# A product of weights whose second operand is loaded twice, once turned, and elementwise work moved up in the planner's order

## Chip, cores, metric

One core of a Trainium2 chip. The metric is the device time of one execution in microseconds, the median of three runs. Engines are named TensorE (PE; its weight loads are PEld), VectorE (DVE), ScalarE (ACT), GpSimd (POOL) and SyncE (SP, which issues most DMAs).

## What is computed

Three blocks in a row, on 2304 tokens of 512 features. First an attention with random features (4 batches, 8 heads, 576 positions, 64 per head, 128 features). Then a normalized, gated feed-forward layer. Then a mixture of eight experts, where every token goes to the expert that a global sort of all token and expert scores assigns to it, at most 288 tokens an expert.

```python
q_p, k_p = phi(q_s), phi(k_s)                  # exp of a projection by omega
kv = einsum('bhsm,bhsd->bhmd', k_p, v);  z = sum(k_p, axis=2)
x = (q_p @ kv) / (q_p @ z + 1e-6)              # then heads side by side: (2304, 512)

xn = x / rms(x) * rms_g
g = xn @ w_gate                                # (512, 1536)
h = g * sigmoid(g) * (xn @ w_val)
x = h @ w_out                                  # (1536, 512)

logits = x @ moe2_w_gate                       # (512, 8)
order = argsort(-logits.flatten())             # greedy: token to expert, 288 each
out[mask_e] = relu(x[mask_e] @ w1[e]) @ w2[e]
```

The weights of the feed-forward layer arrive as 64-bit floats, as pairs of 32-bit words.

## The kernel before

The program is written in a framework that places instructions by a planner. TensorE's order is the program's own during the first part; ScalarE, VectorE, GpSimd and SyncE get theirs from the planner, which simulates the run and gives each engine, among the instructions that it holds ready, the one with the highest priority. Priority is the place in the program; `tc.high_priority(offset=n)` moves a block n instructions ahead. On the chip each engine then works through its list in order. Buffers of a pool are taken and given back as their last reader ends.

Precision: an operand of a big matmul is split into a high part (float32r) and the rest, and three matmuls make one product.

The first part is a loop over 81 ticks, `run_tick`. Each tick works on 76 items of attention (40 for keys, 36 for queries), each item passing through up to six lags, one a tick. In a tick stand, in TensorE's order: the units of weight conversion (`conv_pe`), attention (`it.pe`), and a step of the feed-forward layer's first product (`ffn_step_pe`). From tick 23 on (`FFN_AT`) three ticks of ten have a second step, so there are 1.3 steps a tick. Attention's elementwise work has `AHEAD_A = 200`; that of a step (`ffn_el`) and that of the units (`conv_el`) have no offset.

A unit loads 512 KB of 64-bit weights into one of three "ws" buffers (`load`, always three units ahead). At lag 0 ScalarE takes the magnitude of the upper word (L570), at lag 1 VectorE builds a 32-bit float from the two words with three instructions (L574 to L576, held behind attention's last maximum by `issue_after`). The first 24 units are the gate and value weights: at lag 2 ScalarE and GpSimd split them (L599, L600) into a slab that the steps read. The 12 `WoUnit`s are w_out: at lag 1 the 32-bit float goes to a scratch tensor in HBM (`wo_dr`); at lag 2 TensorE transposes four blocks of 128 by 128 (L614) into a PSUM buffer "gv" and ScalarE copies them back (L629); at lag 3 TensorE multiplies them by the router's weights (L618) into the same buffer, and VectorE copies the 128 by 8 product out in two instructions (L631, L632) as `wog`. So w_out times the router's weights exists, and the router's scores come from h with eight columns (`ffn_lg`). Units start at 0.5 a tick up to tick 23, then 0.9 until all 24 first ones have started, then 0.7.

A step is twelve matmuls (L644, L645, L647) for one slab of 128 of the 1536 features and gate or value, on a block of 512 tokens (four and a half blocks), into a "gv" buffer; the pool has two of them, shared with the units:

```python
psG = ctx.enter_context(tc.tile_pool(name="psG", bufs=2, space=PSUM))
```

After a gate step ScalarE takes tanh (L656) and VectorE multiplies (L657, which gives "gv" back). After a value step VectorE multiplies (L665 in the first block, which then stores h by SyncE at L667; L669 in the others, followed by ScalarE L671, GpSimd L672 and the store L673). A block's first step needs its slab converted (`gvs`), and, one slab later, its `wog` (`wogs`). Steps that are left when attention is done follow in a loop of their own, with `wo_split`, which loads the scratch back and splits it for the second product. After that come the routing, filled with the second product's matmuls, and the experts; the change does not touch them.

Of the kernel before, what the change touches and what calls it, by code (L numbers as in the profile page):

```python
# [9 lines left out]
F32 = mybir.dt.float32  # L10
# [10 lines left out]
NT, DM, FF, E, FE = B * S, 512, 1536, 8, 1024  # L21
# [12 lines left out]
KD = DM // 128  # L34
KF = FF // 128
# [9 lines left out]
DW = 3  # L45
# [5 lines left out]
PACE = (0.5, 0.9, 0.7)  # L51
FFN_AT = 23
AHEAD_A = 200
HB = 6
LATE = 2

# [231 lines left out]


@with_exitstack  # L290
def kernel(ctx, tc, qT, kT, kC, v1, vC, om, wgv, rms, wo, wg2, w1, w2, cfd, trd, cid, out, dbg=None):
    nc = tc.nc
    dbg = dbg or {}
    keep = ctx.enter_context(tc.tile_pool(name="keep", bufs=1))
# [9 lines left out]
    ident = cf[:, C_ID:C_SL]  # L304
# [11 lines left out]
    wg2s = keep.tile([128, KD, E], F32, name="wg2s")  # L316

    xp = ctx.enter_context(tc.tile_pool(name="xp", bufs=2))
    psG = ctx.enter_context(tc.tile_pool(name="psG", bufs=2, space=PSUM))
    mid = ExitStack()  # L320
    fp = mid.enter_context(tc.tile_pool(name="fp", bufs=2))
# [6 lines left out]
    st = {}  # L328
# [73 lines left out]
    class KItem:  # L402
# [42 lines left out]
        def el(self, lag):  # L445
            b, p, g = self.b, self.p, self.g
            if lag == 0:
                self.ft = feat(self.pp, 128, 2 * len(self.ts))
            elif lag == 1 and g == 2:
                r, w = p // 2, b // 2  # L450
                if w not in kvs:
                    kvs[w] = at.tile([128, H, 2, D + 1], F32, name="kvs", bufs=1)
                nc.scalar.copy(kvs[w][:, 4 * r:4 * r + 4, b % 2, :].rearrange("p (o h) d -> p h o d", o=2),
                               st.pop(("pk", b, r))[:, :4 * (D + 1)].rearrange("p (h o d) -> p h o d", h=2, o=2))
# [148 lines left out]
    class WoUnit(Unit):  # L603
# [4 lines left out]
            return wo[self.f]  # L608

        def pe(self, lag):  # L610
            if lag == 2:
                self.pt = psG.tile([128, KD, 128], F32, name="gv")
                for k in range(KD):
                    nc.tensor.transpose(self.pt[:, k, :], self.t[:, k * 128:(k + 1) * 128], ident)  # L614
            elif lag == 3:
                self.pw = self.pt[:, 0, :E]
                for k in range(KD):
                    nc.tensor.matmul(self.pw, self.t[:, k * 128:(k + 1) * 128], wg2s[:, k, :], start=(k == 0), stop=(k == KD - 1))  # L618

        def el(self, lag):  # L620
            f = self.f
            if lag == 0:
                self.magnitude(fp.tile([128, DM], F32, name="dw", bufs=DW))
            elif lag == 1:
                with tc.issue_after(st["mx"].ins):
                    self.word()
                nc.sync.dma_start(wo_dr[f], self.t)
            elif lag == 2:
                nc.scalar.copy(self.t, self.pt.rearrange("p k m -> p (k m)"))  # L629
            elif lag == 3:  # L630
                nc.vector.tensor_copy(wog[:, f, 0, :], self.pw)  # L631
                nc.vector.tensor_sub(wog[:, f, 1, :], self.pw, wog[:, f, 0, :])  # L632
                wogs.add(f)
# [16 lines left out]
    def ffn_el(j, f, v, pg):  # L650
        n = WIDTH[j]
        nh = n // HB2
        if v == 0:
            fst["th"] = fp.tile([128, BLK], F32, name="th")
            th = fst["th"][:, :n]
            nc.scalar.activation(th, pg, AF.Tanh, scale=0.5)  # L656
            nc.vector.scalar_tensor_tensor(th, th, 1.0, pg, op0=OP.add, op1=OP.mult)  # L657
            return
        th = fst["th"][:, :n]
        hp = fp.tile([128, BLK // HB2, 2, HB2], F32R, name="hp")  # L660
        hf = hp.bitcast(F32)
        dst = h_dr[nh * j:nh * j + nh] if nh > 1 else h_dr[NT // HB2 - 1:]
        dst = dst[:, :, f].rearrange("b p x -> p b x")
        if j == 0:
            nc.vector.scalar_tensor_tensor(hf[:, :, 0], pg.rearrange("p (b t) -> p b t", b=nh), 0.5,  # L665
                                           th.rearrange("p (b t) -> p b t", b=nh), op0=OP.mult, op1=OP.mult)
            nc.sync.dma_start(dst[:, :, :HB2], hf[:, :, 0])  # L667
            return
        nc.vector.scalar_tensor_tensor(th, pg, 0.5, th, op0=OP.mult, op1=OP.mult)  # L669
        h = th.rearrange("p (b t) -> p b t", b=nh)  # L670
        nc.scalar.copy(hp[:, :nh, 0], h)  # L671
        nc.gpsimd.tensor_sub(hp[:, :nh, 1], h, hp[:, :nh, 0])  # L672
        nc.sync.dma_start(dst, hf[:, :nh].rearrange("p b l t -> p b (l t)"))  # L673
        fq.append((j, f, hp))
# [30 lines left out]
    def ffn_rank_el():  # L705
        for c0 in rks:
            ranks(nc, st["eng"], fp, cf[:, C_T:C_N].rearrange("p (a b) -> p a b", b=E), L, R, c0, 2)
        rks.clear()
# [14 lines left out]
    def ffn_step_el():  # L723
        if "el" in fst:
            j, f, v, pg = fst.pop("el")
            ffn_el(j, f, v, pg)
            ffn_rank_el()
            return j, f, v
        return None
# [3 lines left out]
    for b in range(B):  # L733
# [1 line left out]
        w, o = divmod(b, 2)  # L735
        items += [QItem(w * PAIR + c, hf) for c in range(o * (PAIR // 2), PAIR // 2 + o * (PAIR // 2 + 1))
                  for hf in range(2)]
    useq = [WgvUnit(f, g) for f in range(KF) for g in range(2)] + [WoUnit(f) for f in range(KF)]
    AHEAD = 3


# [36 lines left out]
    def conv_pe(pace):  # L778
        conv["due"] += pace
        conv["live"] = [(lag + 1, u) for lag, u in conv["live"] if lag < 3]  # L780
        while conv["due"] >= 1 and conv["next"] < len(useq):
            conv["due"] -= 1
            conv["live"].append((0, useq[conv["next"]]))
            conv["next"] += 1
        for lag, u in conv["live"]:
            u.pe(lag)
# [8 lines left out]
    def run_tick(tick):  # L795
        live = [(lag, items[tick - lag]) for lag in range(NLAG) if 0 <= tick - lag < len(items)]
        conv_pe(PACE[0] if tick < FFN_AT else PACE[1] if conv["next"] < 2 * KF else PACE[2])
        with tc.high_priority(offset=AHEAD_A):
            for lag, it in live:
                it.pe(lag)  # L800
        ffn_step_pe()
        for lag, it in live:
            if lag == 5 and isinstance(it, QItem) and it.hf and it.c * 128 // BLK not in xblk:
                while len(xblk) > 1:
                    ffn_step_el()
                    if not ffn_step_pe():
                        conv_el()
                        conv_pe(1)
        with tc.high_priority(offset=AHEAD_A):
            for lag, it in live:  # L810
# [52 lines left out]
    def ffn2_load(c, g):  # L863
        ht = f2.tile([128, 4, 2, 128], F32R, name="ht", bufs=HB)
        j, o = divmod(c * 128, HB2)
# [8 lines left out]
    def late_load(f):  # L874
        hs = f2.tile([128, 4, 2, 128], F32R, name="ht", bufs=HB)
        hs = hs.rearrange("p a l t -> p (a l t)").rearrange("p (b l t) -> p b l t", b=BLK // HB2, l=2)
# [11 lines left out]
    while True:  # L888
# [5 lines left out]
        j, f, v = ffn_step_el()  # L894
# [45 lines left out]
    def ffn2():  # L940
        for i, (c, g) in enumerate(seq2):
            if i + HB - 1 < len(seq2):
                ffn2_load(*seq2[i + HB - 1])
            if i % 6 == 2 and wcur[0] < LOADS:
# [207 lines left out]
def layouts(q, k, v, omega, moe_w_gate, moe_w_val, moe_w_out, moe_rms_g, moe2_w_gate, moe2_w1, moe2_w2):  # L1152
    a = np.asarray
    hp = H // 2

    def bits(x):
        return np.ascontiguousarray(x).view(np.int64)

    qT = a(q).reshape(B, hp, 2, S, D).transpose(2, 4, 1, 0, 3).reshape(128, hp, NC, 128).transpose(2, 0, 1, 3)
    kf = a(k).reshape(B, hp, 2, S, D).transpose(0, 1, 2, 4, 3).reshape(B, hp, 128, S)  # L1160
    kT = kf[..., :512]
    kC = kf[..., 512:].reshape(B, hp // 2, 2, 128, 64).transpose(0, 1, 3, 2, 4).reshape(B, hp // 2, 128, 128)
    vf = np.ones((B, hp, 2, S, D + 1), np.float32)
    vf[..., :D] = a(v).reshape(B, hp, 2, S, D)
    v1 = vf[:, :, :, :512].reshape(B, hp, 2, 4, 128, D + 1).transpose(0, 1, 4, 3, 2, 5)
    vC = np.zeros((B, hp // 2, 2, 64, 2, 2, D + 1), np.float32)
    for o in range(2):
        vC[:, :, o, :, :, o] = vf[:, o::2, :, 512:].transpose(0, 1, 3, 2, 4)
    vC = vC.reshape(B, hp // 2, 128, 2, 2 * (D + 1))
    om = np.zeros((128, 2 * M), np.float32)  # L1170
    om[:D, :M] = a(omega).T
    om[D:, M:] = a(omega).T
    wgv = np.stack([bits(moe_w_gate), bits(moe_w_val)], 0).reshape(2, KD, 128, KF, 128).transpose(3, 2, 0, 1, 4)
    wgv = wgv.reshape(KF, 128, 1024)
    rms = np.tile(a(moe_rms_g)[None], (128, 1))
    wo = bits(moe_w_out).reshape(KF, 128, DM)
    wg2 = a(moe2_w_gate).reshape(KD, 128, E).transpose(1, 0, 2)
    w1 = a(moe2_w1).reshape(E, KD, 128, 4, 256).transpose(0, 3, 2, 1, 4).reshape(E, 4, 128, 1024)
    w2 = a(moe2_w2).reshape(E, KE, 128, KD, 128).transpose(0, 3, 2, 1, 4).reshape(E, 4, 128, 1024)
    d = dict(qT=qT, kT=kT, kC=kC, v1=v1, vC=vC, om=om, wgv=wgv, rms=rms, wo=wo, wg2=wg2, w1=w1, w2=w2,  # L1180
             cf=const_f32(), tri=triangles(), ci=const_i32())
    return {n: np.ascontiguousarray(x) for n, x in d.items()}

# [16 lines left out]
```

## Time and profile before

| what | us |
| --- | --- |
| median of 3 runs | 931.28 |
| lowest, highest | 929.66, 931.54 |
| the profiled execution | 928.5 |
| its span, first to last instruction | 926.7 |

The span is what the profile shows; the rest of an execution lies around it. Busy time of TensorE is the union of its instructions' durations. Matmuls are pipelined, and the end of each is modelled, so one's duration reaches into the next; distances between starts tell what one takes of the engine's order. "Idle before" and the releaser in square brackets, or behind "<-", name what the engine had waited for.

### The profile page before, as it was taken

How to read it: one execution, taken by the hardware profiler on the slowest of the kernel's cores; microseconds unless marked ns; L12 is line 12 of the kernel's file. 1: busy time of each engine (PE TensorE's matmuls, PEld its weight loads, DVE VectorE, ACT ScalarE, POOL GpSimd, SP SyncE). 2: the span in 40 equal slices, each digit the busy share in tenths (PEclk: the TensorE clock that was granted, in tenths of full speed). 3: DMA queues.
4: the chain of work that ended last, by engine and by line, in shares of the span. 5: the costliest groups of instructions: out<-in, count | busy, mean ns of one | idle time of the engine just before them, and what ended most of it. 6: DMA issues, size and time to landing. Idle time of an engine off the chain costs nothing.

```text
span 926.7 us, 16209 instructions
## 1 busy us (share of the span) xinstructions
PE 905.5 (98%) x6219; PEld 786.7 (85%) x6219; DVE 526.7 (57%) x1226; ACT 373.4 (40%) x843; POOL 226.1 (24%) x298
## 2 busy tenths in 40 slices
PE   8998999999999999999999999999999999999996
PEld 7887888888888888877789777777779999999996
DVE  4799895555643354431263666666664665566661
ACT  5985575445544345333242100100013544444441
POOL 1355342122222323255333000000012222122111
PEclk9999999999999999999999999999999999999998
DMA  8556554454322121177674677676623666666650
GB/s 293 180 169 203 147 153 147 143 185 166 127 104 75 61 88 69 46 272 274 194 223 159 193 205 206 190 211 203 182 83 106 181 197 194 187 210 190 185 162 26
DMA packets 111486, 152.61 MB, mean 165 GB/s; under 512 B 6448, under 2 KB 70576, under 8 KB 111408
## 3 DMA queue, kind: packets, MB, share of 16 engines
q1 hardware_dynamic: 105600, 137.28, 47.3%
q0 software_dynamic: 3072, 9.44, 3.3%
q10 hardware_dynamic: 2736, 4.85, 1.4%
q8 instruction: 49, 0.80, 0.4%
q14 instruction: 29, 0.24, 0.1%
HBM read 107.50 MB, written 44.04 MB: 164 GB/s over the span
## 4 chain that ended last, share of the span: by engine, by line
PE 71%; issue 6%; DVE 2%; POOL 2%; DMA 1%; ACT 0%; POOLq 0%; DVEq 0%; ACTq 0%
PE py L955 16%; PE gv L644 8%; PE gv L645 8%; PE gv L647 8%; PE ph L1069 3%; PE ph L1066 3%; PE ph L1067 3%; PE py L1077 3%; PE py L1078 3%; PE py L1079 3%; PE cnt L180 2%; PE pm L496 1%; PE pm L439 1%; PE lg L684 1%; PE gv L618 1%
## 5 line engine op out<-in xcount | busy, mean ns | idle before, releaser
L644 PE MATMUL gv<-xh,wc 128*128 128x512 f32 (+1 forms) x480 | 180.3, 382 | 5.3 <-DVE th L657 4.7
L645 PE MATMUL gv<-xh,wc 128*128 128x512 f32 (+1 forms) x480 | 174.4, 370 | 0.0
L955 PE MATMUL py<-wc,ht 128*128 128x512 f32 x648 | 167.3, 404 | 0.0
L955 PEld LDWEIGHTS py<-wc,ht 128*128 128x128 f32 x648 | 114.9, 189 | 19.0
L647 PE MATMUL gv<-xl,wc 128*128 128x512 f32 (+1 forms) x480 | 118.4, 368 | 0.0
L644 PEld LDWEIGHTS gv<-xh,wc 128*128 128x128 f32 x480 | 90.6, 189 | 23.2 <-DVE th L657 6.3
L645 PEld LDWEIGHTS gv<-xh,wc 128*128 128x128 f32 x480 | 90.6, 189 | 13.7
L647 PEld LDWEIGHTS gv<-xl,wc 128*128 128x128 f32 x480 | 85.3, 189 | 15.7
L657 DVE SCALAR_TENSOR_TENSOR th<-th,gv 128x512 f32<-128x512 f32 (+1 forms) x60 | 37.9, 631 | 104.4 <-ACT th L656 104.1
L399 ACT ACTIVATE ft<-pp,mx 128x128 f32<-128x128 f32 x288 | 82.5, 374 | 18.1 <-DVE mx L396 17.4
L672 POOL TENSOR_TENSOR hp<-th,hp 128x512 fp32r<-128x512 f32 (+1 forms) x48 | 59.8, 1247 | 122.5 <-ACT hp L671 108.6
L926 DVE TENSOR_TENSOR wc<-ws,wc 128x512 fp32r<-128x512 f32 x128 | 84.8, 682 | 0.0
L1077 PE MATMUL py<-ehh,wc 128*128 128x288 f32 x256 | 77.7, 304 | 0.0
L1078 PE MATMUL py<-ehl,wc 128*128 128x288 f32 x256 | 75.9, 297 | 0.0
L1079 PE MATMUL py<-ehh,wc 128*128 128x288 f32 x256 | 75.8, 296 | 0.0
L1066 PE MATMUL ph<-exh,wc 128*128 128x288 f32 x256 | 71.7, 302 | 0.0
L1067 PE MATMUL ph<-exh,wc 128*128 128x288 f32 x256 | 69.8, 295 | 0.0
L966 ACT COPY ys<-py 128x512 f32<-128x512 f32 x18 | 10.6, 588 | 144.3 <-PE py L955 103.5
L936 ACT CAST wc<-ws 128x1024 fp32r<-128x1024 f32 x64 | 66.9, 1046 | 2.4 <-ACT ys L966 2.4
L656 ACT ACTIVATE th<-gv 128x512 f32<-128x512 f32 (+1 forms) x60 | 33.3, 555 | 73.2 <-PE gv L647 64.1
L396 DVE TENSOR_REDUCE mx<-pp 128x4 f32<-128x512 f32 (+1 forms) x76 | 50.0, 657 | 19.0 <-PE pp L392 9.8
L1071 DVE SCALAR_TENSOR_TENSOR ehl<-ph,ehh 128x288 fp32r<-128x288 f32 x64 | 29.3, 458 | 46.8 <-ACT ehh L1070 46.8
(217 smaller groups left out, 1696.4 us busy)
## 6 DMA issues: line engine op xcount, KB each, us to landing
ws<-in_w_dram SPq DMA_DIRECT2D x64, 512.0 KB, 4.0
ht<-h_dr SPq DMA_DIRECT2D x54, 512.0 KB, 4.1
h_dr<-hp SPq DMA_DIRECT2D x36, 512.0 KB, 2.8
ws<-in_wgv_dram SPq DMA_DIRECT2D x24, 512.0 KB, 4.2
h_dr<-hp SPq DMA_DIRECT2D x24, 256.0 KB, 2.5
ws<-in_wo_dram SPq DMA_DIRECT2D x12, 512.0 KB, 3.7
h_dr<-ht SPq DMA_DIRECT2D x12, 512.0 KB, 3.1
y_dr<-ys ACTq DMA_DIRECT2D x18, 256.0 KB, 4.3
```

What stands on the lines that cost most here:

```text
L399: nc.scalar.activation(ft[:n, g], pp[:n, g], AF.Exp, bias=mx[:n, g:g + 1])
L644: nc.tensor.matmul(pg[:, :n], w[:, 0, v, k], xh[:, k, :n], start=(k == 0), stop=False)
L645: nc.tensor.matmul(pg[:, :n], w[:, 1, v, k], xh[:, k, :n], start=False, stop=False)
L647: nc.tensor.matmul(pg[:, :n], w[:, 0, v, k], xl[:, k, :n], start=False, stop=(k == KD - 1))
L926: nc.vector.tensor_sub(w[:, 1, h], sv[:, h], w[:, 0, h])
L936: nc.scalar.copy(w[:, 0], sv)
L955: nc.tensor.matmul(py, ht[:, i4, a], w[:, l, f % 2], start=(f == 0 and n == 0), stop=(f == KF - 1 and n == 2))
L1066: nc.tensor.matmul(ph, w[:, 0, k, m], xh[:, k], start=(k == 0), stop=False)
L1067: nc.tensor.matmul(ph, w[:, 1, k, m], xh[:, k], start=False, stop=False)
L1077: nc.tensor.matmul(py, w[:, 0, k], hh[:, k], start=(k == 0), stop=False)
L1078: nc.tensor.matmul(py, w[:, 0, k], hl[:, k], start=False, stop=False)
L1079: nc.tensor.matmul(py, w[:, 1, k], hh[:, k], start=False, stop=(k == KE - 1))
```

## The change

A second copy of w_out, `woT`, is an input: each of its 12 pieces has the four blocks of 128 by 128 turned. A new `WoTUnit` loads it, makes magnitude and words as before, and at lag 2 multiplies it by the router's weights, with VectorE's two copies in the same lag. The `WoUnit` keeps load, magnitude, words and the store to the scratch tensor, and has no TensorE work any more. The list of units is 24, then 12 `WoTUnit`, then 12 `WoUnit`: 48 for 36. `ffn_el` gets an offset of 150.

```diff
+AHEAD_F = 150
@@ class WoUnit
         def pe(self, lag):
-            if lag == 2:
-                self.pt = psG.tile([128, KD, 128], F32, name="gv")
-                for k in range(KD):
-                    nc.tensor.transpose(self.pt[:, k, :], self.t[:, k * 128:(k + 1) * 128], ident)
-            elif lag == 3:
-                self.pw = self.pt[:, 0, :E]
-                for k in range(KD):
-                    nc.tensor.matmul(self.pw, self.t[:, k * 128:(k + 1) * 128], wg2s[:, k, :], start=(k == 0), stop=(k == KD - 1))
+            pass
 
         def el(self, lag):
             f = self.f
@@
+    class WoTUnit(Unit):
+
+        def __init__(self, f):
+            self.f = f
+
+        def src(self):
+            return woT[self.f]
+
+        def pe(self, lag):
+            if lag == 2:
+                self.pw = psG.tile([128, E], F32, name="gv")
+                for k in range(KD):
+                    nc.tensor.matmul(self.pw, self.t[:, k * 128:(k + 1) * 128], wg2s[:, k, :], start=(k == 0),
+                                     stop=(k == KD - 1))
+
+        def el(self, lag):
+            f = self.f
+            if lag == 0:
+                self.magnitude(fp.tile([128, DM], F32, name="dw", bufs=DW))
+            elif lag == 1:
+                with tc.issue_after(st["mx"].ins):
+                    self.word()
             elif lag == 2:
-                nc.scalar.copy(self.t, self.pt.rearrange("p k m -> p (k m)"))
-            elif lag == 3:
                 nc.vector.tensor_copy(wog[:, f, 0, :], self.pw)
                 nc.vector.tensor_sub(wog[:, f, 1, :], self.pw, wog[:, f, 0, :])
                 wogs.add(f)
@@ def ffn_step_el
-            ffn_el(j, f, v, pg)
+            with tc.high_priority(offset=AHEAD_F):
+                ffn_el(j, f, v, pg)
             ffn_rank_el()
@@
-    useq = [WgvUnit(f, g) for f in range(KF) for g in range(2)] + [WoUnit(f) for f in range(KF)]
+    useq = [WgvUnit(f, g) for f in range(KF) for g in range(2)] + [WoTUnit(f) for f in range(KF)]
+    useq += [WoUnit(f) for f in range(KF)]
@@ layouts
     wo = bits(moe_w_out).reshape(KF, 128, DM)
+    woT = wo.reshape(KF, 128, KD, 128).transpose(0, 3, 2, 1).reshape(KF, 128, DM)
```

## Rows read from the trace of the kernel before

**Rows 1.** The page's head: the span

```profile
span 926.7 us, 16209 instructions
```

**Rows 2.** Five stretches: length, busy time by engine, granted clock, DMA share, GB/s

```profile
57.00:107.00 50.00, 46.74 (x265) 39.90 (x264) 44.91 (x79) 29.34 (x73) 25.71 (x23) 1.00 0.62 188
107.00:150.00 43.00, 42.76 (x259) 37.56 (x258) 36.80 (x73) 28.63 (x71) 19.61 (x23) 1.00 0.47 141
150.00:255.00 105.00, 102.70 (x637) 89.41 (x637) 59.63 (x124) 50.12 (x125) 24.34 (x30) 1.00 0.47 158
255.00:345.00 90.00, 88.59 (x509) 74.88 (x509) 37.16 (x87) 38.70 (x103) 27.40 (x35) 1.00 0.24 84
345.00:505.00 160.00, 159.53 (x910) 132.84 (x909) 62.04 (x130) 58.08 (x120) 61.28 (x73) 1.00 0.52 177
```

**Rows 3.** TensorE's waits from 25 to 275 us: total, times, longest

```profile
PE gv L644 <- DVE th L657: 4.3, 3, 2.7
PE gv L614 <- DVE wog L632: 1.8, 3, 0.6
PE gv L644 <- DVE th L669: 0.3, 1, 0.3
PE gv L644 <- DVE hp L665: 0.3, 1, 0.3
PE gv L614 <- DVE dw L576: 0.2, 1, 0.2
```

**Rows 4.** Timeline: TensorE at one unit: start, length, instructions

```profile
153.23 0.60 PE L614 MATMUL gv<-cf,dw 128*128 128x128 f32 x4
153.58 0.37 PE L387 MATMUL pp<-omh,kh 128*128 128x256 f32 x1
```

**Rows 5.** Groups by line, whole span: busy us, mean ns, idle before

```profile
L614 PE MATMUL gv<-cf,dw 128*128 128x128 f32 x48 | 7.4, 277 | 2.0 <-DVE wog L632 1.8 <-DVE dw L576 0.2
L570 ACT ACTIVATE dw<-ws 128x512 f32<-128x512 f32 x36 | 24.1, 677 | 31.2 <-DMA ws<-in_wgv_dram 13.9 <-issue 9.6 <-PE gv L618 4.4
L574 DVE TENSOR_SCALAR dw<-dw 128x512 int32<-128x512 int32 x36 | 21.4, 596 | 1.6 <-ACT dw L570 1.6
L575 DVE SCALAR_TENSOR_TENSOR dw<-ws,dw 128x512 int32<-128x512 int32 x36 | 32.5, 904 | 0.6
L576 DVE SCALAR_TENSOR_TENSOR dw<-ws,dw 128x512 int32<-128x512 int32 x36 | 27.6, 769 | 0.5
```

**Rows 6.** Timeline: TensorE between a unit's transposes and its matmuls

```profile
256.88 0.60 PE L614 MATMUL gv<-cf,dw 128*128 128x128 f32 x4
...
264.06 0.50 PE L644 MATMUL gv<-xh,wc 128*128 128x512 f32 x1 [1.41 <-DVE th L657]
...
267.41 0.84 PE L618 MATMUL gv<-wg2s,dw 128*128 128x8 f32 x7
```

**Rows 7.** Timeline: ScalarE and VectorE before the longest wait

```profile
70.19 0.63 ACT L656 ACTIVATE th<-gv 128x512 f32<-128x512 f32 x1
...
70.96 1.51 DVE L574 TENSOR_SCALAR dw<-dw 128x512 int32<-128x512 int32 x1
...
75.50 0.67 DVE L657 SCALAR_TENSOR_TENSOR th<-th,gv 128x512 f32<-128x512 f32 x1
```

**Rows 8.** Timeline: the last converted slab (GpSimd) and its reader (TensorE)

```profile
139.71 1.29 POOL L600 TENSOR_TENSOR wc<-dw,wc 128x512 fp32r<-128x512 f32 x1 [2.46 <-ACT wc L599]
...
155.57 0.48 PE L644 MATMUL gv<-xh,wc 128*128 128x512 f32 x1
```

**Rows 9.** Timeline: attention's transposes in the first stretch

```profile
88.16 1.10 PE L485 MATMUL pm<-cf,ft 128*128 128x128 f32 x4 [0.31 <-ACT ft L399]
```

**Rows 10.** Groups by line, VectorE from 57 to 107 us

```profile
L575 DVE SCALAR_TENSOR_TENSOR dw<-ws,dw 128x512 int32<-128x512 int32 x11 | 10.6, 967 | 0.3
L396 DVE TENSOR_REDUCE mx<-pp 128x4 f32<-128x512 f32 (+1 forms) x10 | 6.5, 653 | 0.0
```

**Rows 11.** Waits of SP's queue from 50 to 150 us: total, times, longest

```profile
SPq L667 <- DVE hp L665: 20.6, 8, 7.5
```

More of the change, by code (lines that the diff above doesn't have):

```diff
@@ L290, with kernel @@
 @with_exitstack
-def kernel(ctx, tc, qT, kT, kC, v1, vC, om, wgv, rms, wo, wg2, w1, w2, cfd, trd, cid, out, dbg=None):
+def kernel(ctx, tc, qT, kT, kC, v1, vC, om, wgv, rms, wo, woT, wg2, w1, w2, cfd, trd, cid, out, dbg=None):
     nc = tc.nc
@@ L1179, in layouts @@
     w2 = a(moe2_w2).reshape(E, KE, 128, KD, 128).transpose(0, 3, 2, 1, 4).reshape(E, 4, 128, 1024)
-    d = dict(qT=qT, kT=kT, kC=kC, v1=v1, vC=vC, om=om, wgv=wgv, rms=rms, wo=wo, wg2=wg2, w1=w1, w2=w2,
+    d = dict(qT=qT, kT=kT, kC=kC, v1=v1, vC=vC, om=om, wgv=wgv, rms=rms, wo=wo, woT=woT, wg2=wg2, w1=w1, w2=w2,
              cf=const_f32(), tri=triangles(), ci=const_i32())
```

## The prediction

> **What bounds the kernel now.** I read the page first, for the span [rows 1], then the table of stretches, then the waits of TensorE, then single places in order of time. The table [rows 2] is to be read down its first column. In each of the five stretches TensorE is busy for all but a few microseconds: 3.3 are missing of 50 in the first, 2.3 of 105 in the third, 1.4 of 90 in the fourth, 0.5 of 160 in the fifth. The granted clock is 1.00 in all of them, the 2.4 GHz level. So work taken from TensorE should shorten the span one for one, and the rest to be won is in its waits. [Rows 3] lists these from 25 to 275 us: nearly all are of the first matmul of a feed-forward step (L644) for a PSUM buffer that an elementwise instruction still reads, and of the transposes (L614) for the buffer of the unit before. VectorE is near full in the first two stretches (44.9 of 50 and 36.8 of 43) and far from it later (59.6 of 105, 37.2 of 90).
>
> **The transposes go.** Twelve units of four transposes. One unit's four begin at 153.23 and the next matmul begins at 153.58 [rows 4]: 0.35 us of the order of TensorE, times 12 is 4.2 us. Nothing is put in their place on TensorE; the eight small matmul records of a unit (L618) stay. A transposed result is no longer copied by ScalarE (L629); ScalarE has room (50.1 busy of 105 in the third stretch), so that is worth nothing, and its cover is TensorE itself. How much a transpose costs is the one place where a reading can go wrong: the group of L614 has a mean of 277 ns and a union of 7.4 us [rows 5], but the next matmul starts inside the last one's duration, so the distance between starts is the price.
> The Trainium skill, "TensorE: Matmul & The Clock Gate", Part 4 (PE-mode transpose), gives a transpose of 128 by 128 about 275 ns in a kernel; the trace has 277 for its duration and agrees. Charged so, 48 would be worth an estimated 13.2 us, where the starts give 4.2.
>
> **The buffer is held for less long.** Before, a unit takes one of the two "gv" buffers at lag 2 and gives it back after lag 3, and every feed-forward step needs one too. Two costs follow. The next unit's transposes stand right behind the last unit's matmuls and wait for its VectorE copies: L614 behind L632, 1.8 us in three visits [rows 3]. And when a tick has two steps, both must use the one buffer that is left: in [rows 6] the unit's transposes are at 256.88, its matmuls at 267.41, and the step at 264.06 between them waits 1.41 us for the step before it. The 0.3 behind L669 in [rows 3] I take to be the same. After, the unit's matmuls and their copies lie in one tick, so I count all of it as gained: 1.8 + 1.7 = 3.5 us. At worst the two VectorE copies come late in their tick and the second step of the tick waits for them: then the 1.7 stays. At best no more than 3.5.
>
> **The priority of the elementwise work.** The longest wait of TensorE, 2.7 us, is shown in [rows 7]: ScalarE is done with tanh (L656) at 70.82, but VectorE is in weight conversions, which its order has first, from 70.96 on, and comes to L657 at 75.50. TensorE starts 2.66 us late. With L657 ahead of the conversions that wait is gone, and the 0.3 behind L665 too; the third, of 0.2, stands behind attention's own work, and I leave it: 2.9 us. What becomes late instead? The conversions: but they end far ahead of use. The last slab's lead is 14.6 us (L600 ends at 141.00, the step that reads it starts at 155.57 [rows 8]), and the lead is shortest there, since 0.9 units a tick make 0.45 slabs and the steps use 0.65 (1.3 steps, two a slab). A step's elementwise work on VectorE is 0.7 us, so a conversion's lag grows by a few such. Cost nothing; without this slack it would be TensorE waiting for L600. Second, attention's maxima and exponentials: their offset is 200, now against 150, so some stand behind an elementwise instruction that they went ahead of. In the first stretch attention has no slack: at 88.16 TensorE already waits 0.31 us for an exponential [rows 9]. Ten items have their maxima there [rows 10], so the bounds are 0 and 10 x 0.7 = 7; I take one, 0.7, as the conversions, not attention, are what most of this work passes. Net 2.2 us gained. Third, the words of w_out in the third stretch: [rows 3] has one wait of 0.2 on L576, so some of them have no slack either. They are now read by the small matmuls at the same lag, and may be passed by one elementwise instruction: between 0 and 12 x 0.7 = 8.4 us; as one unit of twelve shows a wait, I take one, 0.7.
>
> **The twelve units added behind.** By the program's paces (0.5, 0.9, 0.7) the units on the turned copy start in ticks 38 to 54, as the old ones did, and the plain ones follow in ticks 55 to 71, of 81: the fourth stretch of [rows 2], which has almost no conversions now. Each adds on ScalarE one 0.68 (L570) and on VectorE 0.60 + 0.90 + 0.77 = 2.27 us (L574 to L576) [rows 5]; that is 27.2 us for VectorE, from 37.2 to 64.4 of 90. Each adds a load of 128 x 512 x 8 bytes; 6.3 MB over 90 us are some 70 GB/s beside the 84 there at a DMA share of 0.24. The twelve stores to the scratch tensor move there too, after these words; what they hold feeds the second product, which comes behind the fifth stretch. TensorE reads nothing of these units. In the second stretch VectorE is 86% busy and TensorE loses 0.24 of 43 us. So 0.3 us; the bound is the next part's.
>
> **A rule against it.** The conversions' second step (L575) has a mean of 967 ns in the first stretch [rows 10], against 904 over all, with GpSimd busy half of the time. In the fourth stretch GpSimd is busy 27.4 us, and if VectorE stood still in all of it while the added words run, it would need 37.2 + 27.2 + 27.4 = 91.8 of 90: full.
> The Trainium skill, "SBUF — State Buffer", Who interferes with whom, says that a VectorE instruction with two SBUF inputs and a GpSimd one that reads SBUF exclude each other for their whole length; the stretched L575 in the rows agrees. It would make the rival "VectorE full" below, not a part of the sum.
>
> **The sum.** -4.2 - 1.8 - 1.7 - 2.2 + 0.7 + 0.3 = -8.9 us. The profiled execution took 928.5 us, 1.8 of it outside its span of 926.7; it would take 919.6. It lies 2.8 under the median shown, 931.28, so I forecast 922.4 for the median, 1.0% faster. With attention at 0 it is 921.7; with half of the ten items late (3.5) and the buffer's 1.7 not gained it is 926.9. This is the likeliest case's own range.
>
> **Rivals.**
> 1. *Attention pays for the priority.* Half of the ten items wait 0.7: the 2.9 is given back with 0.6 more: -4.2 - 3.5 + 0.7 + 0.3 + 0.6 = -6.1, 925.2 us. For it: attention has no slack in the first stretch. Against: the conversions are what stands ahead of L657 there. 0.2.
> 2. *A transpose costs its whole duration.* 7.4 (the union in [rows 5]) for 4.2: -12.1, 919.2 us. Against: [rows 4], the next matmul starts before. The Trainium skill's 275 ns, above, would belong to this case. 0.04.
> 3. *VectorE full in the fourth stretch.* The added words make it like the first, where 3.3 us per 50 are lost: 5.9 over 90, -3.0, 928.3 us. Against: 72% by the mean durations, and the second stretch. 0.06.
> 4. *No change.* The freed time is given back, since a shorter tick leaves the same elementwise chains less cover: 931.3 us. For it: the ticks of the third stretch do lose 2.3 us. Against: those are nearly all the waits listed in [rows 3]. 0.1.
> 5. *Slower: SP's queue.* The stores of h are inside the prioritized block, so SP's order has them sooner. SP waits in order: in 50 to 150 us it waited 20.6 us, eight times, up to 7.5, for L665 [rows 11], and the loads of k, v and q stand behind. If half of the first block's twelve stores hold a load up so that TensorE loses the 2.7 of its longest wait, that is 16.2 us: 931.28 - 8.9 + 16.2 = 938.6. It decides from four stores on (4 x 2.7 = 10.8). Against: with that queue as it is, no wait of TensorE is put down to a DMA. 0.1.
>
> **How the numbers follow.** The likeliest has 0.5, the others as given. Two executions tell apart about 0.2%, 1.9 us, so faster is below 929.4: cases 1 to 3 and the likeliest, 0.8; same 0.1; slower 0.1. The range leaves out the last two: 918 (case 2 less the 1.2 by which it may miss) to 929.5.
>
> **What would show it.** No transposes in the groups of TensorE and some 4 us less busy time before 260 us; no wait on the copies of the product; the waits on L657 and L665 from 57 to 110 us gone, and the conversions' ends nearer to their use. Wrong would be: waits of TensorE on exponentials or on words; VectorE above 85% between 255 and 345; waits on DMAs from 57 to 170 us; or a freed microsecond that the stretches do not show.

## The result, and the profile after

The changed kernel takes 922.14 us (median of 6 runs, 920.2 to 923.74), the one before 929.65 (6 runs, 928.7 to 931.54): ratio 0.9917, 95% interval 0.9906 to 0.9928. That is 7.5 us and lies within 0.3 us of the 922.4 forecast. The forecast was 8.9 us off a base of 931.28, of three runs, which with more runs came out 1.6 lower; so one part of the closeness is chance, and the sum was 1.4 us too large by the medians, which are uncertain by about one microsecond. Which terms were off is what the experiments are for.

The table of stretches of the changed kernel, with the columns of [rows 2] (length, busy time of TensorE, its weight loads, VectorE, ScalarE, GpSimd, granted clock, DMA share, GB/s):

```profile
57.00:107.00 50.00, 46.24 (x256) 38.96 (x255) 43.76 (x75) 28.41 (x71) 25.34 (x22) 1.00 0.61 186
107.00:150.00 43.00, 42.97 (x266) 38.08 (x265) 36.28 (x76) 29.18 (x74) 20.68 (x23) 1.00 0.47 141
150.00:255.00 105.00, 104.25 (x623) 90.31 (x622) 62.66 (x130) 46.43 (x118) 25.01 (x31) 0.98 0.42 138
255.00:345.00 90.00, 90.00 (x517) 76.38 (x516) 63.06 (x120) 44.91 (x117) 31.77 (x37) 1.00 0.51 174
345.00:505.00 160.00, 159.75 (x910) 132.65 (x909) 64.58 (x135) 57.00 (x118) 60.98 (x72) 1.00 0.53 184
```

The third and the fourth stretch lost nearly all their idle time: 0.75 us missing for 2.3, and 0 for 1.4. The fourth took the twelve added units: VectorE 63.1 us for 37.2 (64.4 was reckoned), and TensorE full beside it. The first stretch, where the priority should have told, lost more than before: 3.8 us for 3.3. TensorE's waits from 25 to 275 us, as in [rows 3]:

```profile
PE gv L659 <- DVE th L672: 1.9, 2, 1.0
PE gv L635 <- DVE dw L577: 0.8, 1, 0.8
PE pm L486 <- ACT ft L400: 0.7, 1, 0.7
PE pm L443 <- ACT ft L400: 0.6, 1, 0.6
PE gv L659 <- DVE hp L680: 0.5, 1, 0.5
PE pm L440 <- ACT ft L400: 0.3, 1, 0.3
PE pp L390 <- POOL kl L366: 0.3, 1, 0.3
```

(Lines moved: the step's matmul L644 is L659 now, L657 is L672, the product is L635, the words L575 to L577.) No wait is left on the copies of the product, and none of a step in a tick with two steps. The 2.7 us wait is now 1.0 (0.95 at 74.75), but waits on exponentials of 0.7 and 0.6 are new or larger, another of 1.0 on L672 has come (0.98 at 93.58), and the product waits once, 0.8 us, for its words. How far the matched steps of the feed-forward layer have moved says where the gain lies: at the first step of the second block (167 us) the changed kernel is 0.2 us ahead in these profiles, at the first of the third block (288 us) 5.8, at the end of the layer 6.7. The last 0.9 arises between the 102nd and the 107th of the 120 steps (476 to 485 us before); whose it is comes out below.

### The profile page after: what moved, and what is told of

Read it like the earlier page. It is cut to its first block, busy times and chain, and to the rows that moved or that the text cites. A ratio compares the mean times of both kernels' runs of the same rounds, so it can differ in the third digit from the quotient of the medians.

```text
span 920.2 us, 16173 instructions
## 1 busy us (share of the span) xinstructions
PE 901.9 (98%) x6171; PEld 783.3 (85%) x6171; DVE 554.2 (60%) x1262; ACT 372.8 (41%) x843; POOL 229.8 (25%) x298
## 4 chain that ended last, share of the span: by engine, by line
PE 84%; issue 7%; DVE 5%; POOL 2%; DMA 2%; ACT 1%; SPq 0%; POOLq 0%; ACTq 0%; DVEq 0%
PE py L972 16%; PE gv L659 10%; PE gv L660 10%; PE gv L662 10%; PE pm L497 3%; PE ph L1086 3%; PE ph L1083 3%; PE ph L1084 3%; PE py L1094 3%; PE py L1095 3%; PE py L1096 3%; PE pm L440 2%; PE cnt L181 2%; PE pm L486 2%; PE pp L388 1%
## 5 line engine op out<-in xcount | busy, mean ns | idle before, releaser
L659 PE MATMUL gv<-xh,wc 128*128 128x512 f32 (+1 forms) x480 | 180.9, 383 | 2.5 <-DVE th L672 1.9
L659 PEld LDWEIGHTS gv<-xh,wc 128*128 128x128 f32 x480 | 91.1, 190 | 19.5 <-DVE th L672 3.0
L687 POOL TENSOR_TENSOR hp<-th,hp 128x512 fp32r<-128x512 f32 (+1 forms) x48 | 60.6, 1262 | 114.5 <-ACT hp L686 102.6
L672 DVE SCALAR_TENSOR_TENSOR th<-th,gv 128x512 f32<-128x512 f32 (+1 forms) x60 | 37.9, 632 | 84.4 <-ACT th L671 84.4
```

The lines of the kernel that those rows point to most:

```text
L659: nc.tensor.matmul(pg[:, :n], w[:, 0, v, k], xh[:, k, :n], start=(k == 0), stop=False)
```

## Experiments

Ratios are those to runs of the kernel before on the same chip, with 95% intervals; medians of before were 929.3 to 929.4 in all of them. Differences between two experiments are of medians, and uncertain by one to two microseconds. Distances between the starts of two steps in the profiles are steadier, as long as the granted clock is 1.00 between them: three experiments with the same TensorE work have 116.2 us from the 22nd step to the 46th. They are given in a table below.

**The two parts apart.** The first kernel is the one before with this alone, the second the changed one without it:

```diff
+            with tc.high_priority(offset=AHEAD_F):
+                ffn_el(j, f, v, pg)
```

> The kernel before with the offset of 150 for the elementwise work alone. The prediction's step: 2.9 us of waits behind L657 and L665 go and attention gives back 0.7, so 2.2 us faster than before. The rival (attention pays): the first block's 12 slabs gain nothing on balance, within 1 us of before, with waits on exponentials in the place of those on L657.

> The changed kernel without the offset. If the priority is worth 2.2 us, this is 2.2 slower than the changed kernel, so some 5.5 us faster than before. If attention pays for the priority, this is as fast as the changed kernel, 7 to 8 us faster than before, and the 2.7 us wait on L657 is there as before.

Priority alone: 929.81 us, ratio 1.0008 (0.9996 to 1.002). Turned alone: 921.96, ratio 0.9915 (0.9901 to 0.9929). So the whole gain is the turned weights', and the priority is worth nothing that can be measured, in either company. The waits of TensorE with priority alone, 25 to 290 us:

```profile
PE gv L645 <- DVE th L658: 4.1, 3, 1.8
PE gv L615 <- DVE wog L633: 1.8, 3, 0.6
PE pm L486 <- ACT ft L400: 0.7, 1, 0.7
PE pm L443 <- ACT ft L400: 0.5, 1, 0.5
PE gv L645 <- DVE hp L666: 0.5, 1, 0.5
```

and with the turned weights alone:

```profile
PE gv L659 <- DVE th L672: 2.9, 2, 2.7
PE gv L635 <- DVE dw L577: 0.8, 1, 0.8
PE pm L440 <- ACT ft L400: 0.3, 1, 0.3
PE pp L390 <- POOL kl L366: 0.2, 1, 0.2
PE gv L659 <- DVE hp L680: 0.2, 1, 0.2
```

The priority took the wait of 2.7 down to 0.9; others took the place of the rest, 1.8 us on the same instruction among them. The wait behind the copies of the product (1.8 in three visits) goes with the turned weights only.

**What a transpose costs.** The transposes go back into the changed kernel, in the tick of the product:

```diff
-                self.pw = psG.tile([128, E], F32, name="gv")
+                self.pt = psG.tile([128, KD, 128], F32, name="gv")
+                for k in range(KD):
+                    nc.tensor.transpose(self.pt[:, k, :], self.t[:, k * 128:(k + 1) * 128], ident)
+                self.pw = self.pt[:, 0, :E]
```

> The changed kernel with the four transposes of each unit back on TensorE, in the same tick and into the same buffer as the product, nothing reading them (they are overwritten). By the distance between starts they cost 12 x 0.35 = 4.2 us over the changed kernel; by their durations 7.4 (the union) to 13 us; if TensorE were not the bound there, nothing.

926.89 us, ratio 0.9971 (0.9959 to 0.9983): 4.75 over the changed kernel. Its timeline at one unit:

```profile
156.67 0.60 PE L635 MATMUL gv<-cf,dw 128*128 128x128 f32 x4
...
157.11 0.96 PE L638 MATMUL gv<-wg2s,dw 128*128 128x8 f32 x8
```

The first product matmul starts 0.44 us after the first transpose, though the four are shown as busy for 0.60; 12 x 0.44 is 5.3, and the durations would have asked for 7 or more. The starts are the price. From the 22nd step to the 46th, where the twelve units lie, this kernel takes 121.4 us, 5.2 more than the 116.2 at the same clock.

**What the held buffer costs.** The product is split over two ticks, so that its buffer is held, with no work added:

```diff
+            if lag in (2, 3):
+                for k in ((0,) if lag == 2 else range(1, KD)):
                     nc.tensor.matmul(self.pw, ...
@@ el
-            elif lag == 2:
+            elif lag == 3:
                 nc.vector.tensor_copy(wog[:, f, 0, :], self.pw)
```

> The changed kernel with the product split: the first of its four matmuls at lag 2, the others and the copies at lag 3, so that the buffer is held over a tick as before, with no work added. The prediction's step: 3.5 us slower than the changed kernel (1.8 behind L632 and 1.7 in ticks of two steps). The rival: with prioritized elementwise work the one buffer that is left comes free in time, under 1 us.

924.83 us, ratio 0.9955 (0.9941 to 0.9968): 2.7 over the changed kernel by the medians, 3.5 by the ratios (0.0038 of 929.4). From the 22nd step to the 46th it takes 120.0 us, 3.8 more than 116.2. Its waits:

```profile
PE gv L660 <- DVE th L673: 4.5, 3, 1.8
PE gv L636 <- DVE wog L648: 1.5, 3, 0.6
```

Both kinds are back: 1.5 us behind the copies of the unit before, and the long one in a tick with two steps, 1.73 us at 260.99, in the place of the 1.41 of [rows 6]. Its prioritized elementwise work did not take that away.

**The added units.** The twelve plain units without the three VectorE instructions of their words:

```diff
-                with tc.issue_after(st["mx"].ins):
-                    self.word()
                 nc.sync.dma_start(wo_dr[f], self.t)
```

> The changed kernel whose 12 plain units leave out the three VectorE instructions that build the words, so the second product uses the magnitudes alone. The prediction's step: the added words lie beside TensorE's work and cost 0.3 us. The rival (VectorE full from 255 to 345 us): 3 to 6 us faster than the changed kernel.

922.76 us, ratio 0.9931 (0.9917 to 0.9944): no faster than the changed kernel. From 255 to 345 us VectorE has 37.0 us of 90 for the 63.1, and TensorE is full in both:

```profile
255.00:345.00 90.00, 90.00 (x517) 76.38 (x516) 37.01 (x87) 42.68 (x113) 27.60 (x36) 1.00 0.45 153
```

The added words are hidden; the rival "VectorE full" falls. They were stretched, as the rival had it: in the changed kernel L577 has a mean of 958 ns from 255 to 345 us, where the two words instructions that lay there before took 681 and 693. No reader was held up by it.

**Who pays for the priority.** First, attention's offset at 350 (`AHEAD_A = 350`):

> The changed kernel with attention's offset at 350 instead of 200, so that no prioritized step passes it. If what the priority lost is attention's place (its waits at 84 and 89 us, 0.6 and 0.7), these go and it is 1 to 2 us faster than the changed kernel. If the loss is ScalarE standing at a conversion's load with tanh behind it, the wait of 1.0 at 93.6 us stays and the time is within 1 us of the changed kernel.

924.59 us, ratio 0.9938 (0.992 to 0.9956): 2.4 slower than the changed kernel, which neither case had forecast. The waits on exponentials (0.7 and 0.5) are as they were, and those on L672 rose to 3.4. So attention's place in the order is not what makes them. They do come with the priority of the steps: with the turned weights alone there is none on L486 or L443. TensorE's waits in the changed kernel, in order of time:

```profile
74.75 0.50 PE L659 MATMUL gv<-xh,wc 128*128 128x512 f32 x1 [0.95 <-DVE th L672]
79.51 0.50 PE L659 MATMUL gv<-xh,wc 128*128 128x512 f32 x1 [0.55 <-DVE hp L680]
83.78 0.75 PE L443 MATMUL pm<-vtc,ft 128*128 128x130 f32 x4 [0.56 <-ACT ft L400]
88.74 1.10 PE L486 MATMUL pm<-cf,ft 128*128 128x128 f32 x4 [0.73 <-ACT ft L400]
93.58 0.50 PE L659 MATMUL gv<-xh,wc 128*128 128x512 f32 x1 [0.98 <-DVE th L672]
```

VectorE is busy for 18.8 of the 19 us from 70 to 89 in this kernel, so the first four lie where something that it does sooner puts off something else; that this alone makes them was not tried. For the fifth the list of ScalarE shows a cause. It is in order of time, with the wait in brackets:

```profile
86.97 0.62 ACT L600 CAST wc<-dw 128x512 fp32r<-128x512 f32 x1 [1.77 <-DMA qt<-in_qT_dram]
87.49 0.66 ACT L571 ACTIVATE dw<-ws 128x512 f32<-128x512 f32 x1
88.06 0.35 ACT L454 COPY kvs<-pm 128x260 f32<-128x260 f32 x1
88.31 1.14 ACT L400 ACTIVATE ft<-pp,mx 128x128 f32<-128x128 f32 x4
91.66 0.66 ACT L571 ACTIVATE dw<-ws 128x512 f32<-128x512 f32 x1 [2.20 <-DMA ws<-in_wgv_dram]
92.22 0.58 ACT L671 ACTIVATE th<-gv 128x512 f32<-128x512 f32 x1
```

The tanh at 92.22 belongs to the step that begins at 84.29 and whose last matmul begins before 87.14, when attention's next ones do. Ahead of it in the list is a unit's magnitude (L571), and that stands 2.20 us for its weights to land. VectorE has nothing to do from 89.9 to 92.8, and TensorE waits at 93.58. In the kernel before, this tanh (L656) came ahead of the magnitude (L570):

```profile
88.76 0.61 ACT L656 ACTIVATE th<-gv 128x512 f32<-128x512 f32 x1
90.83 0.68 ACT L570 ACTIVATE dw<-ws 128x512 f32<-128x512 f32 x1 [1.46 <-DMA ws<-in_wgv_dram]
```

With the offset and this order, seven profiles have the wait, of 0.98 to 2.01 us. The next kernel queues each magnitude behind the last tanh emitted before it:

```diff
-            nc.scalar.activation(th, pg, AF.Tanh, scale=0.5)
+            st["th"] = nc.scalar.activation(th, pg, AF.Tanh, scale=0.5)
@@ magnitude
+            with tc.issue_after(st["th"].ins) if "th" in st else ExitStack():
                 nc.scalar.activation(t, self.raw[:, :, 1].bitcast(F32), AF.Abs, scale=W_SCALE)
```

> The changed kernel with each unit's magnitude on ScalarE queued behind the last tanh that was emitted before it, with the program's own way to order one instruction behind another. If the priority's gain was lost because tanh stood behind a magnitude that waited for its load, the wait of 1.0 at 93.6 us goes and it is 1 to 2 us faster than the changed kernel. If not, within 0.5 us, or slower, as the words come later.

918.68 us, ratio 0.989 (0.9875 to 0.9905): 3.5 faster than the changed kernel, of which the order itself gives about half (last section). The same place:

```profile
87.76 1.14 ACT L400 ACTIVATE ft<-pp,mx 128x128 f32<-128x128 f32 x4 [0.30 <-DVE mx L397]
88.77 0.61 ACT L672 ACTIVATE th<-gv 128x512 f32<-128x512 f32 x1
89.25 1.25 ACT L572 ACTIVATE dw<-ws 128x512 f32<-128x512 f32 x2
```

Tanh comes at 88.77, and the wait of TensorE behind it is gone. Whether the offset or the queueing does it is told by the same kernel without the offset:

> The kernel with the magnitude queued behind tanh, without the offset of 150. If the priority is worth the predicted 2 us once tanh doesn't stand behind a late load, this is 2 us slower than with the offset (some 920.7). If the queueing alone brings the gain, or the offset is worth nothing here too, within 1 us of it.

920.81 us, ratio 0.991 (0.9893 to 0.9926): 2.1 slower by the medians than with the offset, and its profile has the wait of 2.7 on the step's product again. The two intervals overlap, so the times alone do not tell them apart. The profiles do. These are distances between the starts of steps in us, of profiles in which the granted clock is 1.00 there (but for the one marked); in the kernel before the 1st step starts at 57.04, the 14th at 114.47, the 22nd at 150.50, the 46th at 275.47, the 102nd at 476.21 and the 107th at 485.38:

| kernel | 1st to 14th step | 22nd to 46th | 102nd to 107th |
| --- | --- | --- | --- |
| before | 57.4 | 125.0 | 9.2 |
| changed | 58.4 | 117.8 (clock 0.98) | 8.3 |
| no added words | 58.8 | 116.2 | 8.3 |
| transposes back | 59.0 | 121.4 | 8.3 |
| buffer held | 59.1 | 120.0 | 8.3 |
| magnitude behind tanh | 56.8 | 116.2 | 8.3 |
| the same, no offset | 57.3 | 116.2 | 9.2 |
| the same with the offset, product at lag 3 (below) | 56.9 | 115.1 | 8.3 |

Where tanh stands behind a late load, the offset costs 0.9 to 1.7 us in the first block; where it doesn't, it gains 0.5. At the end of the layer it gains 0.9 in either company, of which some 0.7 is left at the end of the span. There the kernel before has a wait of 0.35 behind L657, at 478.73; why it is worth more than its length was not tried. So the offset is worth some 1.4 us with tanh in order, by two effects, and about nothing without. That the 2.1 between the medians is near the 2.2 of the forecast is luck: the wait of 2.7 that the forecast priced gives only a part of the 0.5.

**The words of the product.** In the changed kernel the product waits once for its words, and the words were late by one instruction: L576 took 1.66 us while GpSimd ran L687 (1.46 us from 175.52), against 0.69 for L577 behind it.

```profile
175.88 1.66 DVE L576 SCALAR_TENSOR_TENSOR dw<-ws,dw 128x512 int32<-128x512 int32 x1
177.57 0.69 DVE L577 SCALAR_TENSOR_TENSOR dw<-ws,dw 128x512 int32<-128x512 int32 x1
178.31 0.83 PE L635 MATMUL gv<-wg2s,dw 128*128 128x8 f32 x6 [0.75 <-DVE dw L577]
```

With the product and its copies a tick later (`lag == 3` for `lag == 2` in both methods of `WoTUnit`):

> The changed kernel with the unit's whole product and its copies at lag 3 instead of lag 2, in one tick, so the words have a tick more. The one wait for words (0.8 us at 178 us, where the granted clock of the stretch is 0.93) should go: 0.8 us faster than the changed kernel, up to 2.5 if the lower clock goes with it. The rival (the wait is only traded for one a tick later, and nothing depends on it): no difference over 1 us.

920.75 us, ratio 0.9899 (0.9885 to 0.9914): 1.4 faster than the changed kernel, and no wait on L577 is left. The interval overlaps that of the changed kernel. Both improvements together:

> The magnitude queued behind tanh, with the offset, and the product at lag 3. If the two waits (tanh behind a load, product behind words) are separate, their gains add: 1 to 1.5 us faster than the magnitude behind tanh alone, some 917.3. If the second only moves, no difference over 0.7.

917.66 us, ratio 0.9877 (0.986 to 0.9893), 1.0 faster than the magnitude behind tanh alone, which is within the uncertainty of the medians; the table has 1.1 between the 22nd step and the 46th. Against the kernel before it is 11.7 us, against the changed one 4.5, and the intervals of these two do not meet. It is the fastest of all.

## Why the prediction was right, and where it was not

- *The transposes go*, -4.2: right, and somewhat small. Put back, they cost 4.75 by the medians and 5.2 by the steps. The rival of whole durations falls. The 275 ns of the Trainium skill, "TensorE: Matmul & The Clock Gate", Part 4 (PE-mode transpose), agree with the trace as the length of one (272 to 277); its share of TensorE's order is a third of that.
- *The buffer is held for less long*, -3.5: right in kind and size; measured 2.7 by the medians, 3.5 by the ratios, 3.8 by the steps. Both waits named came back when the buffer was held again.
- *The priority of the elementwise work*, -2.2 net: this step failed. Measured, 0 in both companies (1.0008; 922.14 against 921.96). The forecast priced the waits behind L657 and L665 at 2.9 and what becomes late at one exponential, 0.7. Neither came so. The 2.7 us wait fell to 0.95 and the 0.3 behind L665 went, but waits of 0.55, 0.56, 0.73 (0.31 before) and 0.98 came behind them, and from the 1st step to the 14th the changed kernel takes 0.9 us more than the one before, not 2.2 less. I sought what becomes late among the conversions and attention on VectorE; the last of these waits was tanh on ScalarE, one engine earlier in the same step's chain: a unit's magnitude came to stand ahead of it in the list, and that waited for a load. Even with that order mended, the offset gains 0.5 there. The 0.9 that it gains at the end of the layer, and that brings its sum to about 0, stood nowhere in the forecast.
- *Rivals to that step.* "Attention pays" had about the right sum for it. Attention does pay a part, about 1.0 us in two waits on exponentials, but not by its place in the order: its own further offset left them as they were.
- *Conversions have slack*: right. The last slab ends at 142.44 and is read at 157.38, a lead of 14.9 us for the 14.6 of [rows 8].
- *Words of w_out*, +0.7: one unit waited 0.75, but not because a prioritized instruction passed it: the wait is there with the turned weights alone, too. So the size is luck. Taking the wait away gave 1.4 by the medians and 1.1 by the steps.
- *The added units*, +0.3: hidden, no gain without their words.
- *SP's queue*, the rival on the other side: it waited 20.1 us for the value steps, eight times, against 20.6 in [rows 11], and no wait of TensorE is put down to a DMA. What did wait for a DMA was ScalarE.

Together: without the priority the sum forecast -4.2 - 3.5 + 0.7 + 0.3 = -6.7 us, and the turned weights alone measured 7.4 by the medians; from the 22nd step to the 46th, at full clock, their work is shorter by 8.8 (125.0 to 116.2). Transposes and buffer, each put back by itself, cost 5.2 + 3.8 = 9.0 there, so nothing of size is left for a third cause. In medians these two are 4.75 + 2.7 = 7.45, by the ratios 5.0 + 3.5 = 8.5; that the first is so near to the 7.5 of the whole change means little, as each is uncertain by one to two microseconds. The forecast of the whole thus came close in part by luck: the turned weights gave more than their terms, the priority nothing for its 2.2, and the base was 1.6 high.

## What to carry to other kernels

Before a block is given priority, follow its chain over every engine it visits, and look in each in-order list for an instruction that waits for a transfer: an offset in a planner's order can put such a one ahead of the block that was to go first. Look, too, whether the engine that is to work sooner has idle time there: where VectorE had almost none, most of what was gained on a wait of 2.7 us came back as waits of the steps behind it. Price what is taken from a full engine by the distance between starts around it, and the time that a shared buffer is held as an item of its own. Here a second load of an operand in another layout was nearly free, where the memory queues and the converting engines had idle stretches, and it paid twice, as it also shortened the life of a buffer.

## What the hardware showed that I had not expected

A wait of TensorE can be followed by half speed. With the turned weights alone, the wait of 2.7 us ends at 75.63, and the granted clock is 0.50, the 1.2 GHz level, in the five microseconds behind it, in which the matmuls run at half speed (stretches, columns as above):

```profile
70.00:75.00 5.00, 2.94 (x12) 2.12 (x12) 4.97 (x7) 1.68 (x5) 3.42 (x3) 1.00 0.77 255
75.00:80.00 5.00, 4.37 (x10) 3.47 (x11) 4.47 (x8) 3.19 (x7) 2.73 (x3) 0.50 0.59 168
80.00:90.00 10.00, 10.00 (x55) 8.71 (x54) 7.91 (x10) 5.39 (x14) 5.25 (x5) 0.91 0.77 218
```

The kernel before had the same wait with a clock of 1.00 in that stretch, and the changed kernel had 0.98 from 150 to 255 us, where its wait of 0.75 lies. The clock falls in some executions and not in others: the changed kernel's six runs have mean clocks from 0.993 (923.74 us) to 0.998 (920.2 us). The experiment "magnitude behind tanh" has the same wait of 0.75 us at 176.45, and its clock stays. First the changed kernel, then that one:

```profile
180.00:184.00 4.00, 4.00 (x18) 3.35 (x17) 0.97 (x2) 2.10 (x6) 0.73 (x1) 0.62 0.48 180
180.00:184.00 4.00, 4.00 (x26) 3.40 (x25) 1.51 (x3) 1.20 (x5) 0.58 (x1) 1.00 0.18 66
```

From the 22nd step to the 46th the one takes 117.8 us and the other 116.2, with the same work: the fall costs 1.6. So of the 3.5 us between these two profiled executions (922.03 and 918.54) 1.6 is the clock, and 1.6 more the first block (58.4 to 56.8), which is what the order of tanh gives. A wait taken away may take some of the lower clock with it; that the wait causes the fall is not shown, as three profiles have the wait of 0.75 and a clock of 1.00 behind it. In four others (priority alone, transposes back, attention further, product at lag 3) the clock is 0.72 from 10 to 16 us, where the kernels do the same, and their first step begins at 58.7 to 59.0 us instead of 56.4 to 57.6.
